# One fused kernel on one core: second block in halves, fewer float64 steps among the experts, expert 0's weights loaded later

## Chip, cores and metric

The kernel runs on one core of one Trainium2 chip. The metric is the device time of one launch in microseconds. Before the change the median of three runs is 641.63 us.

## What is computed

Three stages follow each other, on 2 x 768 tokens of 512 features.

```
x = attention(q, k, v)          # 2 batches, 8 heads, 768 positions, 64 features a head;
                                # a query sees the first n_global=8 keys and the last n_local=96
e = argmax(x @ w_gate); y = gate * relu(x @ w1[e]) @ w2[e]     # 8 experts, 512 -> 1024 -> 512
h = y @ w_in; g = max(h, 0) + log1p(exp(-|h|)); out = g @ w_out  # 512 -> 2048 -> 512, w_in, w_out float64
```

## The kernel before

**Attention.** The loop at L960 has one step `n` for each of 12 tiles x 8 heads (tile `i`, head `h`), plus eight steps to drain. A tile is 128 queries; tiles 0 and 6 are the first of a batch and see only their own keys, the others also the 96 keys before and the 8 global ones. In step `n` the scores of head `n` are multiplied (L720), the probabilities of head `n-4` transposed (L747), and in odd steps the heads `n-7` and `n-6` multiplied by v (L768). For the older keys L768 reads `vp`, which GpSimd fills in step 7 of the tile before (`prev_v`, L561 to L571; in a batch's second tile L570 also copies the global rows). q, k and v are loaded by SyncE (`load` at h = 1, `load_v` at h = 6). Each finished tile is routed (`route`, L792): x is transposed (L798, in step 8x+15), the expert chosen, and in step 8x+20 GpSimd scales the rows (L847) and scatters them to DRAM by an indirect DMA (L788, `scatter_x`). A scatter waits for the one before it. From tile 3 on there is a scatter in that step; step 7 of tiles 5, 6 and 7 issues one more, to catch up.

**Expert 0's parts.** L1011 calls `pump(-1, 0)` at step 4 of tiles 6 and 8; each call issues one half of expert 0's weights, two DMAs of 1 MB each (L405, L406, on SyncE's queue).

**Experts.** The loop at L1146 has 64 steps `s` (8 experts x 8 slices of the 1024 inner units) and two to drain: stage 1 of slice `s` (L1110), stage 2 of slice `s-2` (L1126). `pump` loads the weights of coming experts into five buffers. After four loads for the second block `load_x` (L1064) brings the last expert's rows, transposed at L1091.

**float64 weights.** `w_in` and `w_out` come as float64 words. `conv_step` (L487) turns one of 64 pieces (128 x 256) into float32: one store to DRAM (L492), one bit operation on VectorE (L80), one on ScalarE (L76) and two on VectorE (L77, L78), one load of a coming piece (L484). It runs twice a tile in attention from tile 5, once in each expert step from s = 6 (L1164), and twice in each step of the second block.

**Second block.** 1536 tokens in 3 chunks of 512, 2048 inner units in 8 blocks of 256, q0 to q7 (`Q2 = 8`). A step `x` of the plan (L1229) is one of 48 = 3 chunks x 16 slices: 12 matmuls of stage 1 (L1095 to L1097 through `three`, since each operand is split into a high and a low part), then 12 of stage 2 for step `x-2`. Chunk by chunk all 8 blocks are walked, forward, backward, forward. A block must be split into high and low before use: two raw loads (L462), four copies (L431 or L433) and four subtractions (L421). With five buffers, 14 blocks are loaded and split instead of 8. The output of a chunk stays in four PSUM banks through its 16 steps; `m_out` (L1215) then copies it (L1220 ScalarE, L1222 VectorE in turn) and scatters the rows to `out` (L1223). The last six steps run row block by row block (L1245).

What sets the order is the program: each engine takes its instructions in the order in which these loops issue them, and SyncE's and ScalarE's DMAs wait in those queues.

```
        if n in (6 * H + 4, 8 * H + 4):
            pump(-1, 0)
...
        if s >= 6:
            conv_step(1)
...
        return conv_done[0] >= 8 * (key[2] + 1)
```

Of the kernel before, what the change touches and what calls it, by code (L numbers as in the profile page):

```python
# [10 lines left out]
F32 = mybir.dt.float32  # L11
F32R = mybir.dt.float32r
# [4 lines left out]
ALU = mybir.AluOpType  # L17
# [5 lines left out]
P = 128  # L23
# [282 lines left out]
def fast_path(ctx, tc, q, k, v, n_global, n_local, w_gate, w1, w2, cap, w_in, w_out, out, const):  # L306
    nc = tc.nc
    B, H, S, D = q.shape
    T, DM = out.shape
    E, _, F = w1.shape  # L310
    F2 = w_in.shape[1]
# [3 lines left out]
    NTT = T // P  # L315
# [4 lines left out]
    Q2 = F2 // FQ  # L320
# [13 lines left out]
    rpool = ctx.enter_context(tc.tile_pool(name="rpool", bufs=3))  # L334
    cv = ctx.enter_context(tc.tile_pool(name="cv", bufs=2))

    xp = ctx.enter_context(tc.tile_pool(name="xp", bufs=1))
# [8 lines left out]
    uses = []  # L346
    for e in range(E):
        uses += [("e", e, i) for i in range(QE)]
    for c in range(T // 512):
        order = range(Q2) if c % 2 == 0 else range(Q2 - 1, -1, -1)  # L350
        uses += [("m", 0, i) for i in order]

    slot_of = {}
    use_buf = [None] * len(uses)
# [29 lines left out]
    NRAW = 4  # L384
# [95 lines left out]
    def conv_load():  # L480
        if conv:
            src, dst = conv.popleft()
            raw = cv.tile([P, FQ, 2], I32, name="cr", tag="cr", bufs=4)
            nc.scalar.dma_start(raw.rearrange("p n w -> p (n w)"), src)  # L484
            conv_raw.append((raw, dst))

    def conv_step(n):  # L487

        for _ in range(n):
            if conv_out:  # L490
                dst, t = conv_out.popleft()
                nc.scalar.dma_start(dst, f32(t))  # L492
                conv_done[0] += 1
            if conv_now:
                dst, t, u = conv_now
                words_to_f32(nc, t, u, None, None, 1)
                conv_out.append((dst, t))
                conv_now.clear()
            if conv_raw:
                raw, dst = conv_raw.popleft()  # L500
                t = cv.tile([P, FQ], I32, name="ct", tag="cq", bufs=5)
                u = cv.tile([P, FQ], F32, name="csq", tag="cu", bufs=2)
                words_to_f32(nc, t, u, raw[:, :, 1], raw[:, :, 0], 0)
                conv_now.extend([dst, t, u])
                conv_load()
# [454 lines left out]
    for n in range(NH + 8):  # L960
        i, h = divmod(n, H)
        if 0 <= n - 2 < NH:
            expo(n - 2)
        if 0 <= n - 1 < NH:
            if n <= H:
                make_bias0(n - 1)
            biased(n - 1)
            if n <= H:
                make_bias1(n - 1)
        if n < NH:  # L970
            scores(n)
        if 0 <= n - 4 < NH:
            transp(n - 4)
        if n % 2:
            for m in (n - 7, n - 6):
                if 0 <= m < NH:
                    pv(m)
        if n == H + 2:
            tri = strict_upper(nc, const, "tri", a2, ints, tag="here")
        if n < NH:  # L980
            if h == 1:
                load(i + 2)
            if h == (1 if i else 3):
                prep(i + 1, 0)
            if h % 2 and (i or h > 4) or i and h == 2:
                zero_fill(1)
            if h == (3 if i else 5):
                prep(i + 1, 1)
            if h == 6:
                load_v(i + 2)  # L990
                if i in (2, 3, 4):
                    conv_load()
            if h == 7:
                dup(i + 1)
                prev_v(i + 1)
                if i >= 5 and len(sc_q) > (i > 10):
                    scatter_x()
            if i >= 5 and h >= 6 and i < last:
                conv_step(1)
        for step, off in enumerate((15, 18, 20)):  # L1000
            x, r = divmod(n - off, H)
            if r == 0 and 0 <= x < last - 1:
                route(x, step)
        for step, at in enumerate((NH - 1, NH + 3, NH + 5)):
            if n == at:
                route(last - 1, step)
        if n == (last - 2) * H + 21:
            assert not sc_q
            moe_x["xr"] = ac.tile([P, 2, DM], F32, name="xr0")
            nc.sync.dma_start(moe_x["xr"], xs_d[0:FIRST, :].rearrange("(j p) d -> p j d", p=P))  # L1010
        if n in (6 * H + 4, 8 * H + 4):  # L1011
            pump(-1, 0)
    first_base(0)
    route(last, 0)
# [125 lines left out]
    LAG = 2  # L1140
# [5 lines left out]
    for s in range(len(steps) + LAG):  # L1146
        if s < len(steps):
            ui, f = steps[s]
            e_stage1(ui, f)
            if f in (3, 5, 6):  # L1150
                trans_x(ui + 1, (3, 5, 6).index(f))
            if f == 7 or s == 0:
                if s == 0:
                    load_order()
                load_x(ui + 1 + (f == 7))
        if s >= LAG:
            ui, f = steps[s - LAG]
            e_stage2(ui, f)
            if f % JE == JE - 1:
                done = ui * QE + f // JE  # L1160
        pump(done, 2 if s > 2 else 0, s % 2 == 0)
        if 1 <= s <= 4:
            next(routed, None)
        if s >= 6:  # L1164
            conv_step(1)


    NCH = T // 512
    plan = []
    for c in range(NCH):  # L1170
        for s in range(Q2):
            u = UM + c * Q2 + s
            for j in range(2):
                plan.append((c, u, 2 * s + j, j))
    NF2 = F2 // P
    gs_, os_ = {}, {}

    def m_stage1(x):
        c, u, f, j = plan[x]
        w = w_of(u)[0]  # L1180
        ps = bank("A", "ps_m")
        sl = slice(c * 512, (c + 1) * 512)
        for d in range(NC):
            three(ps, w[:, 0, d, j * P:(j + 1) * P], w[:, 1, d, j * P:(j + 1) * P], zh[:, d, sl], zl[:, d, sl],
                  d == 0, d == NC - 1)
        a = cv.tile([P, 512], F32, name="sa", tag="sa", bufs=2)
        nc.scalar.activation(a, ps, AF.Abs)  # L1187
        nc.scalar.activation(a, a, AF.Exp, scale=-1.0)
        nc.scalar.activation(a, a, AF.Ln, bias=1.0)  # L1189
        nc.vector.scalar_tensor_tensor(a, in0=ps, scalar=0.0, in1=a, op0=ALU.max, op1=ALU.add)  # L1190
        y = x - (len(plan) - TAIL)
        if 0 <= y < 4:
            if y % 2 == 0:
                gs_["two"] = (mo if y // 2 else xp).tile([P, 4, 512], F32R, name="g2", tag=f"x{y // 2}", bufs=1)
            gh, gl_ = gs_["two"][:, y % 2, :], gs_["two"][:, 2 + y % 2, :]
        else:
            g = mo.tile([P, 2, 512], F32R, name="g", tag="h", bufs=3)
            gh, gl_ = g[:, 0, :], g[:, 1, :]
        nc.vector.tensor_copy(gh, a)  # L1199
        nc.vector.tensor_tensor(gl_, a, f32(gh), op=ALU.subtract)  # L1200
        gs_[x] = (gh, gl_)

    def m_stage2(x, ts_=range(4)):
        c, u, f, j = plan[x]
        w = w_of(u)[1]
        if f == 0:
            os_[c] = [bank("BBCC"[t], "ps_o") for t in range(4)]
        gh, gl_ = gs_[x]
        for t in ts_:
            three(os_[c][t], gh[:, t * P:(t + 1) * P], gl_[:, t * P:(t + 1) * P], w[:, 0, j, :], w[:, 1, j, :],  # L1210
                  f == 0, f == NF2 - 1)
            if f == NF2 - 1:
                m_out(c, t)

    def m_out(c, t):  # L1215
        if t % 2 == 0:
            os_[c, "o"] = mo.tile([P, 2, 512], F32, name="o", tag="m4", bufs=2)
        o = os_[c, "o"][:, t % 2, :]
        if t % 2:
            nc.scalar.copy(o, os_[c][t])  # L1220
        else:
            nc.vector.tensor_copy(o, os_[c][t])  # L1222
        nc.gpsimd.indirect_dma_start(  # L1223
            out=out, out_offset=bass.IndirectOffsetOnAxis(ap=ids_sb[:, 4 * c + t:4 * c + t + 1], axis=0), in_=o,
            in_offset=None, bounds_check=T - 1, oob_is_err=False)
# [2 lines left out]
    slow = None  # L1228
    for x in range(len(plan)):  # L1229
        m_stage1(x)  # L1230
        conv_step(1)
        if LAG <= x < len(plan) - TAIL + LAG:
            m_stage2(x - LAG)
            if (x - LAG) % 2 == 1:
                done = plan[x - LAG][1]
        conv_step(1)
        pump(done, 2)
        if x < NTT:
            scatter_ids(x)
        if x == NTT:  # L1240
            nc.sync.dma_start(ids_sb, ids_d.rearrange("(j p) o -> p (j o)", p=P))
        if x == 2 * NF2:
            slow = nc.values_load(slow_i[0:1, 0:1], min_val=0, max_val=1,
                                  skip_runtime_bounds_check_because="one minus a minimum of comparisons")
    for t in range(4):  # L1245
# [46 lines left out]
```

## Time and profile before

| | us |
|---|---|
| median of 3 runs | 641.63 |
| lowest, highest run | 638.79, 643.66 |
| the profiled execution, its own time | 643.61 |
| its span | 641.7 |
| TensorE matmul busy in the span | 622.5 |
| VectorE, ScalarE, GpSimd busy | 308.1, 266.9, 122.6 |

The span is what the profile shows; 1.9 us of the execution's time lie around it. Attention fills about the first 150 us of the span, the experts reach to about 367, the second block to the end.

### The profile page before, as it was taken

The numbers are of one execution on the slowest core, as the hardware profiler recorded it, in microseconds if no ns is written. First come the engines' busy times: TensorE is split into PE (matmuls) and PEld (weight loads), VectorE is DVE, ScalarE is ACT, GpSimd is POOL, SyncE is SP. The second block draws the span as 40 slices with busy tenths as digits, with TensorE's granted clock in tenths as the row PEclk, the third lists the DMA queues.
The fourth block names the chain that finished last, engine by engine and source line by source line (L and its number), as shares of the span: only waits on it lengthen the run. The fifth ranks groups of instructions, "written<-read, shape, count | busy, mean of one in ns | idle before, by whom it ended". The sixth has DMA issues, their size and how long they took to land. (4 is left out here: it accounts for less than half of the span.)

```text
span 641.7 us, 9519 instructions
## 1 busy us (share of the span) xinstructions
PE 622.5 (97%) x3257; PEld 535.9 (84%) x3257; DVE 308.1 (48%) x939; ACT 266.9 (42%) x570; POOL 122.6 (19%) x152
## 2 busy tenths in 40 slices
PE   6999979999999999999999999999999999999996
PEld 4899979998876788999989978888888888888874
DVE  7766868955031233343466354533345433455340
ACT  4565746742222223333344354433445333344340
POOL 3231443311000000000022432531042100142001
PEclk9999979989999999999999999999999999999999
DMA  8758898413995677899996432540023200011001
GB/s 170 209 173 228 228 271 268 148 51 112 386 387 193 190 254 277 288 316 316 309 345 200 148 48 34 105 71 12 1 95 93 76 0 1 33 66 34 1 1 69
DMA packets 94666, 99.61 MB, mean 155 GB/s; under 512 B 44790, under 2 KB 60162, under 8 KB 94610
## 3 DMA queue, kind: packets, MB, share of 16 engines
q1 hardware_dynamic: 73874, 67.45, 36.7%
q10 hardware_dynamic: 18432, 25.17, 11.6%
q0 software_dynamic: 2304, 6.30, 2.6%
q8 instruction: 28, 0.46, 0.3%
q14 instruction: 28, 0.23, 0.1%
HBM read 78.44 MB, written 20.46 MB: 154 GB/s over the span
## 5 line engine op out<-in xcount | busy, mean ns | idle before, releaser
L1126 PE MATMUL ps_y<-h,w 128*128 128x256 f32 (+7 forms) x512 | 115.0, 368 | 0.0
L1110 PE MATMUL ps_h<-xT,w 128*128 128x256 f32 (+7 forms) x512 | 114.7, 368 | 0.0
L1110 PEld LDWEIGHTS ps_h<-xT,w 128*128 128x128 f32 x512 | 93.3, 190 | 12.1 <-ACT xT L1080 0.2
L1126 PEld LDWEIGHTS ps_y<-h,w 128*128 128x128 f32 x512 | 92.0, 190 | 10.7
L1190 DVE SCALAR_TENSOR_TENSOR sa<-ps_m,sa 128x512 f32<-128x512 f32 x48 | 33.2, 692 | 132.7 <-ACT sa L1189 132.7
L1187 ACT ACTIVATE sa<-ps_m 128x512 f32<-128x512 f32 x48 | 28.8, 600 | 137.3 <-PE ps_m L1097 136.2
L1112 ACT ACTIVATE h<-ps_h 128x256 f32<-128x256 f32 (+7 forms) x64 | 23.8, 373 | 139.7 <-PE ps_h L1110 120.1
L1095 PE MATMUL ps_m<-zh,w1s 128*128 128x512 f32 x192 | 75.9, 395 | 0.0
L1097 PE MATMUL ps_o<-w2s,g 128*128 128x512 f32 x192 | 75.7, 394 | 0.0
L1096 PE MATMUL ps_m<-zl,w1s 128*128 128x512 f32 x192 | 75.7, 394 | 0.0
L1096 PE MATMUL ps_o<-w2s,g 128*128 128x512 f32 x192 | 75.5, 393 | 0.0
L1097 PE MATMUL ps_m<-zh,w1s 128*128 128x512 f32 x192 | 75.3, 392 | 0.0
L1095 PE MATMUL ps_o<-w2s,g 128*128 128x512 f32 x192 | 74.8, 389 | 0.0
L80 DVE SCALAR_TENSOR_TENSOR ct<-csq,ct 128x256 int32<-128x256 int32 x64 | 29.2, 457 | 78.0 <-ACT csq L76 76.7
L421 POOL TENSOR_TENSOR w1s<-raw,w1s 128x512 fp32r<-128x512 f32 x19 | 24.9, 1321 | 212.6 <-ACT w1s L433 212.5
L736 ACT ACTIVATE s_sb<-s_sb,negm 128x232 f32<-128x232 f32 (+1 forms) x96 | 44.7, 473 | 36.7 <-DVE negm L729 36.1
L720 PE MATMUL ps_s<-kwin,qpad 128*128 128x232 f32 (+1 forms) x192 | 56.4, 381 | 2.1 <-DVE negm L729 2.0
L1095 PEld LDWEIGHTS ps_m<-zh,w1s 128*128 128x128 f32 x192 | 36.0, 188 | 9.3 <-DVE sa L1190 1.0
L1096 PEld LDWEIGHTS ps_o<-w2s,g 128*128 128x128 f32 x192 | 36.0, 188 | 8.7
L1095 PEld LDWEIGHTS ps_o<-w2s,g 128*128 128x128 f32 x192 | 36.1, 188 | 8.4 <-DVE g L1199 0.3
L1097 PEld LDWEIGHTS ps_m<-zh,w1s 128*128 128x128 f32 x192 | 36.0, 188 | 8.4
L1097 PEld LDWEIGHTS ps_o<-w2s,g 128*128 128x128 f32 x192 | 36.0, 188 | 8.1 <-DVE g L1200 0.4
(185 smaller groups left out, 919.3 us busy)
## 6 DMA issues: line engine op xcount, KB each, us to landing
w<-in_moe_w_dram SPq DMA_DIRECT2D x32, 1024.0 KB
cr<-in_moe_w_in_dram ACTq DMA_DIRECT2D x32, 256.0 KB
cr<-in_moe_w_out_dram ACTq DMA_DIRECT2D x32, 256.0 KB
raw<-wi_d SPq DMA_DIRECT2D x14, 512.0 KB
raw<-wo_d SPq DMA_DIRECT2D x14, 512.0 KB
xs_d<-early SPq DMA_DIRECT2D x22, 256.0 KB
wi_d<-ct ACTq DMA_DIRECT2D x32, 128.0 KB
wo_d<-ct ACTq DMA_DIRECT2D x32, 128.0 KB
```

Of the source, the lines that this page charges most:

```text
L80: nc.vector.scalar_tensor_tensor(t, in0=u.bitcast(I32), scalar=3, in1=t, op0=ALU.logical_shift_left, op1=ALU.bitwise_or)
L421: eng.tensor_tensor(lo, raw, f32(hi), op=ALU.subtract)
L720: nc.tensor.matmul(ps[:, :w], tr[i][h % 2][:, h // 2, :], kwin[t % 2][:, h // 2, c0:], start=True, stop=True)
L736: nc.scalar.activation(pt_[n][:, :w], pt_[n][:, :w], AF.Exp, bias=negm[:, n:n + 1], scale=-1.0)
L1095: nc.tensor.matmul(ps, hi_l, hi_r, start=first, stop=False)
L1096: nc.tensor.matmul(ps, hi_l, lo_r, start=False, stop=False)
L1097: nc.tensor.matmul(ps, lo_l, hi_r, start=False, stop=last)
L1110: nc.tensor.matmul(ps, w[:, c, j * P:(j + 1) * P], xt_[ui][:, c, :], start=c == 0, stop=c == NC - 1)
L1112: nc.scalar.activation(h[:, :n], ps, AF.Relu)
L1126: nc.tensor.matmul(ys[ui, d], w[:, j, d * P:(d + 1) * P], h, start=f == 0, stop=f == NFE - 1)
L1187: nc.scalar.activation(a, ps, AF.Abs)
L1190: nc.vector.scalar_tensor_tensor(a, in0=ps, scalar=0.0, in1=a, op0=ALU.max, op1=ALU.add)
```

## The change

- The second block is walked in halves of the inner units. `segs` lists six segments of 8 steps: chunks 0, 1, 2 with blocks q0 to q3, then chunks 2, 1, 0 with q4 to q7. In this order each block is loaded and split once (8 instead of 14).
- Chunk 2 keeps its PSUM banks through both halves. Chunks 0 and 1 are copied to SBUF after their first half (`m_keep`, ScalarE and VectorE in turn), and `m_out` adds that copy on VectorE at the end of their second half.
- Among the experts `conv_step` runs in even steps only, in the second block once a step.
- `load_v` is called at h = 5 instead of 6 (the `conv_load` of tiles 2 to 4 stays at h = 6).
- Expert 0's two parts are pumped at step 4 of tiles 9 and 10 instead of 6 and 8.
- The four `g` tiles of the tail use the buffers of the raw loads.

```diff
+    segs = []
+    for half in range(2):
+        for c in range(NCH) if half == 0 else range(NCH - 1, -1, -1):
+            qs = range(half * Q2 // 2, (half + 1) * Q2 // 2)
+            segs.append((c, half, qs if (len(segs) + half * NCH) % 2 == 0 else qs[::-1]))
+    for _, _, qs in segs:
+        uses += [("m", 0, i) for i in qs]
...
-            if h == 6:
+            if h == 5:
                 load_v(i + 2)
-                if i in (2, 3, 4):
-                    conv_load()
+            if h == 6 and i in (2, 3, 4):
+                conv_load()
...
-        if n in (6 * H + 4, 8 * H + 4):
+        if n in (9 * H + 4, 10 * H + 4):
             pump(-1, 0)
...
-        if s >= 6:
+        if s >= 6 and s % 2 == 0:
             conv_step(1)
...
         if 0 <= y < 4:
+            g = rpool.tile([P, 2, 512], F32R, name="g2", tag="raw", bufs=NRAW)
...
+        on = c == NCH - 1
+        if first and not (on and half):
             os_[c] = [bank("BBCC"[t], "ps_o") for t in range(4)]
...
             three(os_[c][t], gh[:, t * P:(t + 1) * P], gl_[:, t * P:(t + 1) * P], w[:, 0, j, :], w[:, 1, j, :],
+                  first and not (on and half), end and not (on and not half))
+            if end and half:
                 m_out(c, t)
+            elif end and not on:
+                m_keep(c, t)
...
+        if t == 0:
+            kept[c] = (mo if c else xp).tile([P, 4, 512], F32, name="kept", tag=f"x{c}", bufs=1)
+        if t % 2:
+            nc.scalar.copy(kept[c][:, t, :], os_[c][t])
+        else:
+            nc.vector.tensor_copy(kept[c][:, t, :], os_[c][t])
...
+        if c in kept:
+            nc.vector.tensor_tensor(o, os_[c][t], kept[c][:, t, :], op=ALU.add)
+        elif t % 2:
...
         m_stage1(x)
-        conv_step(1)
         if LAG <= x < len(plan) - TAIL + LAG:
```

## Rows read from the trace of the kernel before

**Rows 1.** The page's first part: busy time, share, instructions of each engine.

```profile
PE 622.5 (97%) x3257; PEld 535.9 (84%) x3257; DVE 308.1 (48%) x939; ACT 266.9 (42%) x570; POOL 122.6 (19%) x152
```

**Rows 2.** Waits of TensorE in the span: total us, times, longest.

```profile
PE ps_pv L768 <- POOL vp L571: 3.1, 1, 3.1
...
PE ps_xt L1091 <- DMA xr<-xs_d: 1.6, 1, 1.6
```

**Rows 3.** Stretches of 4 us; columns as in the first line.

```profile
core 0: us, PE busy (x) PEld busy (x) DVE busy (x) ACT busy (x) POOL busy (x), PEclk, DMA share, GB/s
...
84.00:88.00 4.00, 1.63 (x12) 1.27 (x10) 3.86 (x18) 2.81 (x7) 1.40 (x2) 0.95 1.23 266
88.00:92.00 4.00, 3.30 (x14) 3.18 (x15) 1.21 (x4) 0.44 (x1) 3.18 (x3) 0.50 0.75 246
...
112.00:116.00 4.00, 4.00 (x34) 3.76 (x33) 3.88 (x12) 2.91 (x7) 3.26 (x4) 1.00 0.54 154
...
140.00:144.00 4.00, 4.00 (x22) 4.00 (x22) 3.10 (x24) 1.11 (x3) 0.00 (x0) 0.50 0.01 2
```

**Rows 4.** A stretch of 40 us of the second block, same columns.

```profile
380.00:420.00 40.00, 40.00 (x175) 32.54 (x174) 20.20 (x31) 17.68 (x30) 14.21 (x12) 1.00 0.47 82
```

**Rows 5.** Timeline of TensorE: the transposes of L798, one set a tile.

```profile
67.61 0.61 PE L798 MATMUL ps_xT<-ident,x 128*128 128x128 f32 x4
...
76.88 0.61 PE L798 MATMUL ps_xT<-ident,x 128*128 128x128 f32 x4
...
90.47 1.06 PE L798 MATMUL ps_xT<-ident,x 128*128 128x128 f32 x4
...
103.07 0.61 PE L798 MATMUL ps_xT<-ident,x 128*128 128x128 f32 x4
...
113.74 0.60 PE L798 MATMUL ps_xT<-ident,x 128*128 128x128 f32 x4
```

**Rows 6.** Timeline of GpSimd: start, us; in brackets the idle time before.

```profile
72.25 0.98 POOL L788 DMA_INDIRECT xs_d<-xg,sl  x1 [3.00 <-DMA xs_d<-xg,sl]
...
79.19 1.02 POOL L788 DMA_INDIRECT xs_d<-xg,sl  x1 [2.49 <-DMA xs_d<-xg,sl]
...
86.58 1.40 POOL L570 COPY vp<-vt 8x520 f32<-8x520 f32 x2 [5.84 <-issue]
88.03 0.61 POOL L571 COPY vp<-vt 96x520 f32<-96x520 f32 x1
```

**Rows 7.** Scatters of L788, issue to landing: all twelve, the one at 72.3, the one at 79.2.

```profile
DMA to landing us min/median/max: 2.7/4.9/7.3
...
DMA to landing us min/median/max: 6.2/6.2/6.2
...
DMA to landing us min/median/max: 7.3/7.3/7.3
```

**Rows 8.** Timeline of SyncE's queue in attention.

```profile
72.77 0.39 SPq L405 DMA_DIRECT2D w<-in_moe_w_dram  x1
...
96.42 0.39 SPq L406 DMA_DIRECT2D w<-in_moe_w_dram  x1
...
113.62 0.31 SPq L540 DMA_DIRECT2D vt<-in_v_dram  x1
...
136.20 0.39 SPq L1010 DMA_DIRECT2D xr<-xs_d  x1
```

**Rows 9.** SyncE's waits from 300 to 420 us, and its timeline there.

```profile
SPq L462 <- DMA wi_d<-ct: 6.4, 1, 6.4
...
326.44 1.09 SPq L1072 DMA_DIRECT2D xr<-xs_d  x2
```

**Rows 10.** Groups of instructions in the second block: busy us, mean ns.

```profile
L1190 DVE SCALAR_TENSOR_TENSOR sa<-ps_m,sa 128x512 f32<-128x512 f32 x48 | 33.2, 692 | 132.7 <-ACT sa L1189 132.7
...
L421 POOL TENSOR_TENSOR w2s<-raw,w2s 128x512 fp32r<-128x512 f32 x15 | 19.4, 1296 | 31.0 <-ACT w2s L433 14.3 <-issue 6.4 <-SPq L1258 5.3
...
L1220 ACT COPY o<-ps_o 128x512 f32<-128x512 f32 x6 | 3.5, 582 | 15.0 <-PE ps_o L1097 15.0
```

More of the change, by code (lines that the diff above doesn't have):

```diff
@@ L348, in fast_path @@
         uses += [("e", e, i) for i in range(QE)]
-    for c in range(T // 512):
-        order = range(Q2) if c % 2 == 0 else range(Q2 - 1, -1, -1)
-        uses += [("m", 0, i) for i in order]
+    NCH = T // 512
+    segs = []
[5 more added lines that the diff above has]
+        uses += [("m", 0, i) for i in qs]
     slot_of = {}
@@ L1163, in fast_path @@
             next(routed, None)
-        if s >= 6:
+        if s >= 6 and s % 2 == 0:
             conv_step(1)
-    NCH = T // 512
     plan = []
-    for c in range(NCH):
-        for s in range(Q2):
-            u = UM + c * Q2 + s
+    for k, (c, half, qs) in enumerate(segs):
+        for i in range(len(qs)):
             for j in range(2):
-                plan.append((c, u, 2 * s + j, j))
-    NF2 = F2 // P
+                e = 2 * i + j
+                plan.append((c, half, UM + k * len(qs) + i, j, e == 0, e == 2 * len(qs) - 1))
     gs_, os_ = {}, {}
     def m_stage1(x):
-        c, u, f, j = plan[x]
+        c, _, u, j = plan[x][:4]
         w = w_of(u)[0]
@@ L1192, in m_stage1 @@
         if 0 <= y < 4:
-            if y % 2 == 0:
-                gs_["two"] = (mo if y // 2 else xp).tile([P, 4, 512], F32R, name="g2", tag=f"x{y // 2}", bufs=1)
-            gh, gl_ = gs_["two"][:, y % 2, :], gs_["two"][:, 2 + y % 2, :]
+            g = rpool.tile([P, 2, 512], F32R, name="g2", tag="raw", bufs=NRAW)
         else:
             g = mo.tile([P, 2, 512], F32R, name="g", tag="h", bufs=3)
-            gh, gl_ = g[:, 0, :], g[:, 1, :]
+        gh, gl_ = g[:, 0, :], g[:, 1, :]
         nc.vector.tensor_copy(gh, a)
@@ L1203, in m_stage2 @@
     def m_stage2(x, ts_=range(4)):
-        c, u, f, j = plan[x]
+        c, half, u, j, first, end = plan[x]
         w = w_of(u)[1]
-        if f == 0:
+        on = c == NCH - 1
+        if first and not (on and half):
             os_[c] = [bank("BBCC"[t], "ps_o") for t in range(4)]
@@ L1210, in m_stage2, with m_keep @@
             three(os_[c][t], gh[:, t * P:(t + 1) * P], gl_[:, t * P:(t + 1) * P], w[:, 0, j, :], w[:, 1, j, :],
-                  f == 0, f == NF2 - 1)
-            if f == NF2 - 1:
+                  first and not (on and half), end and not (on and not half))
+            if end and half:
                 m_out(c, t)
+            elif end and not on:
+                m_keep(c, t)
+    kept = {}
+    def m_keep(c, t):
+        if t == 0:
[4 more added lines that the diff above has]
+            nc.vector.tensor_copy(kept[c][:, t, :], os_[c][t])
     def m_out(c, t):
@@ L1218, in m_out @@
         o = os_[c, "o"][:, t % 2, :]
-        if t % 2:
+        if c in kept:
+            nc.vector.tensor_tensor(o, os_[c][t], kept[c][:, t, :], op=ALU.add)
+        elif t % 2:
             nc.scalar.copy(o, os_[c][t])
@@ L1234, in fast_path @@
             if (x - LAG) % 2 == 1:
-                done = plan[x - LAG][1]
+                done = plan[x - LAG][2]
         conv_step(1)
@@ L1241, in fast_path @@
             nc.sync.dma_start(ids_sb, ids_d.rearrange("(j p) o -> p (j o)", p=P))
-        if x == 2 * NF2:
+        if x == 2 * NTT:
             slow = nc.values_load(slow_i[0:1, 0:1], min_val=0, max_val=1,
```

## Prediction, made before the result was known

> **What bounds the kernel now.** I read the page's first part, then stretches, then TensorE's waits, then the timelines around the longest wait. TensorE is busy for 622.5 of 641.7 us [rows 1], so an edit that only unloads VectorE, ScalarE, GpSimd or the DMAs saves nothing by itself: only idle TensorE time, and time at the lower clock, can be had. In the second block there is none. Five stretches of 40 us from 380 to 580 each show 40.00 busy with 175 matmuls, two chunk ends among them [rows 4]. A step of 24 matmuls takes 24 x 40/175 = 5.49 us, and the change keeps all 48 steps. The two waits of TensorE that the change can reach are 3.1 us in attention, for `vp`, and 1.6 us among the experts, for rows from DRAM [rows 2].
>
> The first is dearer than it looks. In 84 to 88 us TensorE is busy for 1.63 of 4 us, and in the next 4 us its granted clock is 0.50, the lower level, 1.2 GHz [rows 3]. The transposes of L798 come once a tile and measure it: a full tile takes 113.74 - 103.07 = 10.67 us, the light one at the change of batch 76.88 - 67.61 = 9.27, but the two around the wait 13.59 and 12.60 [rows 5]. The first of these is partly light too, so I hold it against 9.27: 4.32 + 1.93 = 6.25 us lost; against 10.67 for both it would be 4.85.
>
> **Expert 0's parts moved.** Why was `vp` late? L571 ended at 88.64; TensorE had wanted it from 88.7 - 3.1 = 85.6. L571 stands behind L570 on GpSimd, which began at 86.58 after 5.84 us for which the profile names no releaser [rows 6]. The scatter issued at 79.19 took 7.3 us to land [rows 7], so it landed at 86.5, 0.1 us earlier. I take that as the releaser: the next scatter must wait for it, and the wait seems to have been placed ahead of the copies. That scatter had itself waited for the one of 72.25, which took 6.2 us [rows 6, 7]. Right there, at 72.77, SyncE issued the first 2 MB of expert 0 [rows 8]; in 84 to 88 the DMA share is 1.23 [rows 3].
>
> Without those 2 MB, with a landing time L for both scatters: the second is issued at 72.25 + L + 0.74 (79.19 less 78.45), lands L later, and the copies are done 0.1 + 2.06 us after that: 75.15 + 2L. TensorE waits only if this passes 85.6, so if L is over 5.2. The median of the twelve is 4.9, from 2.7 to 7.3 [rows 7], and the slow end lies beside this load. I take L = 4.9, no wait, and with no wait no lower clock there: -6.25 us. Bounds: 0 (L near 7) and -6.25.
>
> What do the parts cost at tiles 9 and 10? On SyncE's queue the first now comes behind tile 11's q and k and just ahead of its v load, which is issued at 113.62 before the change [rows 8]; the second follows at once, because SyncE runs ahead and nothing of tile 10 is left to load. Ahead of the next user of that queue, the load at 136.20 [rows 8], lie over 20 us; 4.2 MB at the 266 GB/s of a crowded stretch need 16, and in 112 to 116 only 154 GB/s are moved [rows 3]. v of tile 11 is read 18 steps, or 24 us (10.67/8 a step), after its issue. The scatters there come a tile (10.67 us) apart, without a second one on their heels, so one of 7.3 us still lands before the next. The nearest evidence is the old second part, its last DMA issued at 96.42 [rows 8]: the tile after it took its 10.67 us [rows 5]. So 0, with 0 and 6.25 per tile (what the old first part cost) as ends; nothing could be gained there, as TensorE doesn't idle in it.
>
> One rule of the Trainium skill speaks against this edit. The page "DMA: Bandwidth & Descriptors", section "Issuing engines are not separate DMA queues", says that DMAs started by SyncE, ScalarE or GpSimd end up on the same 16 engines and interleave. The slow scatter beside SyncE's load agrees (7.3 against 2.7 us). By the rule alone the delay only moves, to the scatters of tiles 9 and 10, and the sum below would lack its first term.
>
> **v loads one step earlier.** The order of SyncE's DMAs is the same (a zero-fill of step 5 before, one of step 7 behind), and the load waits for the same products with v, of step 5. 0, within 0.3 either way, a tenth of the one wait for `vp`.
>
> **float64 steps thinned among the experts.** Of TensorE's idle time there only the 1.6 us count [rows 2]; freed VectorE and ScalarE time saves nothing. The late rows are loaded at 326.44, behind a raw load before which SyncE stood 6.4 us for a float64 store [rows 9]. With a store every second step that store lies further back and the DMAs are emptier; a load a few us earlier removes the wait. I take -1.6, between 0 and -1.6.
>
> The price is lateness. Attention converts 12 pieces and the experts 30 more instead of all 52. A block needs 8 pieces more than the one before it, and a piece is stored two calls after its first. q0 to q3 are stored by s = 48 and q4 by s = 64, before use; q7 by x = 23, is split at x = 24 and 25 and used from x = 30: 5 x 5.49 = 27 us to spare. q5 and q6 are stored before their buffers come free, and have about as much. ScalarE may stand at a copy whose raw load has just been issued, which costs nothing as it works some 16 of 40 us [rows 4]. 0; each step of lateness past x = 30 would cost 5.5.
>
> **Halves; each block split once.** Six blocks less are 24 copies and 24 subtractions less, of up to 1.296 us on GpSimd [rows 10]. They lie beside TensorE's unbroken work [rows 4]: 0. New are eight copies (`m_keep`) and eight additions. Chunk ends at which banks are reused go from two to four. Between a chunk's last matmul and the first that needs its third bank lie 12 + 6 matmuls, 4.1 us; four additions in a row on VectorE at 0.692 (nearest: L1190, which also reads PSUM and SBUF [rows 10]) are 2.8 us, most of it while the banks are still being filled. 0; without that cover one addition at each of four ends, 2.8. On the path to the end stands only the last one: 0.692 in place of ScalarE's 0.582 [rows 10], +0.1.
>
> **Sum.** From the profiled execution's own 643.61 us (span 641.7 and 1.9 around it): -6.25 - 1.6 + 0.1 gives 635.9. That execution lies 2.0 above the median, 641.63, near the top of runs from 638.79 to 643.66. A second stretch at the lower clock, 140 to 144 [rows 3], isn't touched; it costs about 3 us (half of some 6) where it occurs, and could make part of that spread. I can't tell how much of the 2.0 the changed kernel keeps, and take 0.5 off: 635.4 us.
>
> **Rivals.**
> - *The wait shrinks only.* With L = 6.2, as at 72.25, the copies end at 87.55 and TensorE waits 2.0 instead of 3.1 us; in proportion 4.0 of the 6.25 stay: 639.4. For it: L must stay under 5.2 and its median is 4.9, twice in a row. Against: 6.2 was reached with the load in flight. 0.18.
> - *The loads hurt at the new place.* If `vp` or v of tiles 10 and 11 comes late at both as it did at tile 7, 12.5 us come on top: 647.9, slower than before. It decides where a scatter holds the copies past TensorE's need; with one scatter a tile instead of two back to back, one landing of some 6 us less stands in the way. 0.05. The section of the Trainium skill named above leads here.
> - *The late rows stay late*, because SyncE is held by something else: 637.0. 0.10.
> - *The second stretch at the lower clock goes too*, since the tail of attention falls 6 us earlier: 632.4. The profile can't tell. 0.12.
> - *The halves and the single split do what they say and move no time*: part of the forecast. That they cost, by 2.8 us at the chunk ends, would give 638.2, and lies within the range.
>
> **How the numbers follow.** The forecast has 0.55, its own range 633.5 to 637. A measurement of this kernel tells about 1% from no change, that is 6.4 us: 635.2 and 648.0. Faster by over 1%: somewhat under half of the forecast and its bounds to the low side (0.28) and the rival at 632.4 (0.12), 0.40. Slower by over 1%: the upper half of the second rival and what I have not thought of, 0.04. The rest, 0.56, is within 1%. The range 631 to 641 takes in all but the rival at 647.9 and the outer ends.
>
> **What would show it.** Right: no idle TensorE between 75 and 95 us with a clock of 1.00, L798's intervals 9.3 and about 10.7 in place of 13.59 and 12.60; no wait at L1091; 175 matmuls in every 40 us of the second block; L421 32 times instead of 56. Wrong: a wait for `vp` or ps_pv after 100 us; TensorE idle at a chunk end or at L1095 for a split; the lower clock at a new place.

## Result, and the profile after

The changed kernel is slower, by half a per cent: median 645.01 us of 22 runs against 641.50 of 22 of the kernel before, ratio 1.0051, 95% interval [1.0028, 1.0074]. Forecast was 635.4, from 631 to 641. The profiled execution of the changed kernel took 644.8 us (span 642.9) against 643.61 (641.7). Function for function the new line numbers are 4 to 18 higher: L804 is the old L798, L577 the old L571, L1101 to L1103 the three matmuls, L1191 to L1194 the old L1187 to L1190, L1258 the load of `ids_sb`.

I cut both traces at the first matmul of the experts, at the first of the second block and at the last of all. Attention got shorter by 5.0 us (it ends at 146.27 instead of 151.28), the experts by 1.3 (216.32 instead of 217.64), and the second block longer by 7.4 (273.85 instead of 266.45). The second stretch at the lower clock, at the end of attention, lasted 6.8 us in both. So the gain came, and something unforeseen took more back. The page's first part answers [rows 1]: as much TensorE work, less on the other engines.

```profile
PE 622.3 (97%) x3257; PEld 535.6 (83%) x3257; DVE 300.0 (47%) x933; ACT 256.7 (40%) x552; POOL 102.0 (16%) x136
```

TensorE's waits over the whole span answer [rows 2]:

```profile
PE ps_m L1101 <- DVE sa L1194: 5.4, 1, 5.4
PE ps_prep L698 <- POOL vp L610: 4.1, 1, 4.1
...
PE ps_xt L1097 <- DMA xr<-xs_d: 0.3, 1, 0.3
```

The 3.1 us for `vp` at the old L768 are gone, the 1.6 us for the late rows have become 0.3, and there is a new wait of 5.4 us at the first matmul of a step of the second block, for VectorE. (The 4.1 us of the second line lie at the start of the kernel and are there before the change too.) Around tile 7, to be read against [rows 3, 5], with the same columns:

```profile
80.00:84.00 4.00, 3.45 (x28) 3.03 (x26) 3.71 (x16) 1.79 (x6) 1.07 (x2) 1.00 0.93 242
84.00:88.00 4.00, 4.00 (x29) 3.68 (x30) 3.43 (x21) 3.10 (x9) 3.38 (x4) 1.00 0.40 114
88.00:92.00 4.00, 4.00 (x33) 3.82 (x33) 3.31 (x12) 2.77 (x7) 2.09 (x3) 1.00 0.90 257
```

```profile
77.26 0.61 PE L804 MATMUL ps_xT<-ident,x 128*128 128x128 f32 x4
...
87.38 0.60 PE L804 MATMUL ps_xT<-ident,x 128*128 128x128 f32 x4
...
98.06 0.60 PE L804 MATMUL ps_xT<-ident,x 128*128 128x128 f32 x4
```

The clock stays at 1.00, and the two intervals are 10.12 and 10.68 us instead of 13.59 and 12.60. Stretches of the second block, to be read against [rows 4]:

```profile
core 0: us, PE busy (x) PEld busy (x) DVE busy (x) ACT busy (x) POOL busy (x), PEclk, DMA share, GB/s
380.00:420.00 40.00, 40.00 (x175) 32.49 (x174) 23.47 (x51) 16.81 (x31) 7.21 (x7) 1.00 0.61 102
...
424.00:428.00 4.00, 4.00 (x19) 3.26 (x18) 2.08 (x5) 0.00 (x0) 0.97 (x1) 1.00 0.05 2
428.00:432.00 4.00, 4.00 (x19) 3.23 (x19) 0.00 (x0) 0.00 (x0) 0.97 (x1) 1.00 0.01 0
432.00:436.00 4.00, 3.12 (x14) 2.22 (x12) 0.00 (x0) 0.00 (x0) 0.00 (x0) 1.00 0.14 1
436.00:440.00 4.00, 0.00 (x0) 0.00 (x0) 0.22 (x1) 2.11 (x5) 0.00 (x0) 0.70 0.69 199
440.00:444.00 4.00, 3.47 (x8) 2.80 (x9) 3.69 (x9) 2.30 (x5) 0.00 (x0) 0.50 0.47 135
444.00:448.00 4.00, 4.00 (x18) 3.24 (x18) 2.19 (x5) 2.18 (x4) 0.00 (x0) 0.94 0.28 94
448.00:488.00 40.00, 40.00 (x175) 32.52 (x174) 24.76 (x49) 18.95 (x35) 4.16 (x3) 1.00 0.27 83
```

Read it down the columns of zeros: ScalarE does nothing from 424 to 436, VectorE nothing from 428 to 436, TensorE nothing from 436 to 440, and then TensorE runs at the lower level, 1.2 GHz. On both sides of the hole stand the 175 matmuls of before. ScalarE stood for 14.3 us, 11 more than the up to 3.3 that it idles in a step; matmuls whose operands were ready hid some 5.6 of them. The price is the rest, 5.4 us, and nine matmuls at the lower clock (3.97 us from the first to the tenth instead of 2.08, so 1.9), together 7.3 of the 7.4 us by which the block is longer.

Who stood first? The timeline of ScalarE (ACTq is its DMA queue):

```profile
422.61 0.63 ACT L1193 ACTIVATE sa<-sa 128x512 f32<-128x512 f32 x1
422.67 0.33 ACTq L498 DMA_DIRECT2D wi_d<-ct  x1
423.15 0.41 ACT L76 ACTIVATE csq<-cr 128x256 f32<-128x256 f32 x1
437.45 0.34 ACTq L490 DMA_DIRECT2D cr<-in_moe_w_in_dram  x1
437.83 0.60 ACT L1191 ACTIVATE sa<-ps_m 128x512 f32<-128x512 f32 x1 [14.26 <-DMA ids_sb<-ids_d]
```

The activation at 437.83 is named as the waiting instruction, but ahead of it in the same queue stands the load of the next float64 piece (L490), which `conv_step` issues. In the steps around it such a load goes out within 0.7 us of the store (L498); here 14.8 us behind it. The profile names as releaser (what ended the wait) a DMA with which this load has no data in common: the load of the token numbers, `ids_sb`, which SyncE issues. SyncE's queue shows when:

```profile
402.30 0.36 SPq L468 DMA_DIRECT2D raw<-wo_d  x1
433.21 0.36 SPq L1258 DMA_DIRECT2D ids_sb<-ids_d  x1
```

and its waits from 360 to 460 us why:

```profile
SPq L1258 <- DMA ids_d<-tokid,pos_i: 30.5, 1, 30.5
```

`ids_sb` must wait for the twelve scatters of `scatter_ids`, one after the other on GpSimd. First and last of them:

```profile
370.18 1.26 POOL L927 DMA_INDIRECT ids_d<-tokid,pos_i  x1 [0.16 <-issue]
...
430.15 0.97 POOL L927 DMA_INDIRECT ids_d<-tokid,pos_i  x1 [2.28 <-DMA ids_d<-tokid,pos_i]
```

In the records of the two DMAs the link can be read. Each DMA signals a completion semaphore, a counter that tells when its data has landed. Both DMAs signal the same one, number 105, and ahead of the ScalarE load at 437.45 stands a wait for it. The last signal of the `ids_sb` load comes at 437.37, and the wait ends within 0.05 us of that. In this program semaphores 101 to 108 are given to the DMAs of SyncE and of ScalarE together, and a DMA that gets a number waits until its last holder has landed, whichever engine issued that; the DMAs of GpSimd signal 111 to 118. The kernel before has the same load and a wait of SyncE for the same scatters:

```profile
SPq L1241 <- DMA ids_d<-tokid,pos_i: 15.6, 1, 15.6
```

But there ScalarE issues no DMA in the second block, since all 64 pieces were converted before it.

Theory A: this coupling is the whole loss, and a gain of the forecast's size lies behind it. Against it stood that the halves, the thinned conversion or the moved loads cost time in themselves. Theory D concerns the other side: that the wait for `vp` was worth less than I had put it at, because it is not in every execution of the kernel before.

### The profile page after: what moved, and what is told of

It reads as the page before. It is cut to its first block, busy times and chain, and to the rows that moved or that the text cites. A ratio compares the mean times of both kernels' runs of the same rounds, so it can differ in the third digit from the quotient of the medians.

```text
span 642.9 us, 9399 instructions
## 1 busy us (share of the span) xinstructions
PE 622.3 (97%) x3257; PEld 535.6 (83%) x3257; DVE 300.0 (47%) x933; ACT 256.7 (40%) x552; POOL 102.0 (16%) x136
## 5 line engine op out<-in xcount | busy, mean ns | idle before, releaser
L1194 DVE SCALAR_TENSOR_TENSOR sa<-ps_m,sa 128x512 f32<-128x512 f32 x48 | 33.2, 691 | 124.8 <-ACT sa L1193 124.8
L1191 ACT ACTIVATE sa<-ps_m 128x512 f32<-128x512 f32 x48 | 28.8, 600 | 144.8 <-PE ps_m L1103 130.6
L1101 PE MATMUL ps_m<-zh,w1s 128*128 128x512 f32 x192 | 76.8, 400 | 5.4 <-DVE sa L1194 5.4
L1103 PE MATMUL ps_m<-zh,w1s 128*128 128x512 f32 x192 | 76.0, 396 | 0.0
L1103 PE MATMUL ps_o<-w2s,g 128*128 128x512 f32 x192 | 75.7, 394 | 0.0
L1101 PE MATMUL ps_o<-w2s,g 128*128 128x512 f32 x192 | 74.7, 389 | 0.0
L80 DVE SCALAR_TENSOR_TENSOR ct<-csq,ct 128x256 int32<-128x256 int32 x64 | 31.2, 488 | 80.4 <-ACT csq L76 80.1
L427 POOL TENSOR_TENSOR w1s<-raw,w1s 128x512 fp32r<-128x512 f32 x11 | 15.2, 1391 | 260.6 <-ACT w1s L439 260.6
L1101 PEld LDWEIGHTS ps_m<-zh,w1s 128*128 128x128 f32 x192 | 36.6, 190 | 15.2 <-DVE sa L1194 6.8
L1103 PEld LDWEIGHTS ps_m<-zh,w1s 128*128 128x128 f32 x192 | 36.4, 190 | 8.6
L1102 PEld LDWEIGHTS ps_o<-w2s,g 128*128 128x128 f32 x192 | 36.0, 188 | 8.7
L1101 PEld LDWEIGHTS ps_o<-w2s,g 128*128 128x128 f32 x192 | 36.1, 188 | 8.4 <-DVE g L1201 0.3
L1102 PEld LDWEIGHTS ps_m<-zl,w1s 128*128 128x128 f32 x192 | 36.4, 190 | 7.9
```

Source lines behind the costliest of these rows:

```text
L80: nc.vector.scalar_tensor_tensor(t, in0=u.bitcast(I32), scalar=3, in1=t, op0=ALU.logical_shift_left, op1=ALU.bitwise_or)
L427: eng.tensor_tensor(lo, raw, f32(hi), op=ALU.subtract)
L1101: nc.tensor.matmul(ps, hi_l, hi_r, start=first, stop=False)
L1102: nc.tensor.matmul(ps, hi_l, lo_r, start=False, stop=False)
L1103: nc.tensor.matmul(ps, lo_l, hi_r, start=False, stop=last)
```

## Experiments on the loss

**1. Conversion in each expert step again**, so that ScalarE has no load left in the second block:

```diff
-        if s >= 6 and s % 2 == 0:
+        if s >= 6:
             conv_step(1)
```

> The changed kernel with the float64 step back in every step among the experts (the rest of the change stays). Theory A: in the changed kernel ScalarE stands 14.3 us in the second block because its load of a float64 piece has to wait for the load of the row numbers (ids_sb), which itself waits for twelve scatters; TensorE loses 7.4 us by it (second block 273.9 us against 266.5 before). With all pieces converted before the second block ScalarE issues no DMA there: no wait at the softplus, second block 266.5, about 645.0 - 7.4 = 637.6 us. Rival B: the halves and the copies of partial sums cost the 7.4 us: the wait stays and the time is about 645.

637.57 us, ratio to the kernel before 0.9947 [0.9918, 0.9976]. The second block takes 266.46 us, ScalarE's waits hold no DMA, and SyncE's waits from 360 to 460 us are:

```profile
SPq L468 <- DVE w1s L427: 60.0, 2, 49.3
SPq L1258 <- DMA ids_d<-tokid,pos_i: 48.2, 1, 48.2
```

SyncE stands at `ids_sb` even longer, 48.2 us instead of 30.5, and the second block is as short as before the change. So it isn't SyncE's wait that costs, but what hangs on its end. The wait for late rows is 1.9 us here.

**2. The load of `ids_sb` later**, when ScalarE's last load has long gone out (458.62):

```diff
-        if x == NTT:
+        if x == 26:
             nc.sync.dma_start(ids_sb, ids_d.rearrange("(j p) o -> p (j o)", p=P))
```

> The changed kernel with the load of the row numbers issued at x = 26 instead of 12, after the last float64 piece (x = 23) and before its first use (x = 33); the thinned float64 steps stay. Theory A: the wait is gone although the pieces are still converted in the second block: second block 266.5, about 637.6 us. Rival C: it is the float64 work itself in the second block (ScalarE, VectorE and DMA time between the softplus) that costs: the time stays near 645 here, while the kernel with the steps back among the experts is faster.

635.39 us (634.03 to 638.21), 0.9913 [0.9882, 0.9944]: one number in one line takes 9.6 us off the changed kernel by the medians, and 8.9 by the two ratios (the kernel before has a median of 641.50 beside the result and of 640.24 here). The load is issued at 488.69, where the scatters are long done, and the second block takes 266.44 us. TensorE has no listed wait left in it. ScalarE's waits from 360 to 460 us:

```profile
ACT sa L1191 <- PE ps_m L1103: 47.0, 16, 3.3
ACT csq L76 <- DVE ct L77: 2.5, 3, 1.2
ACT sa L1191 <- DVE ct L80: 2.0, 1, 2.0
```

ScalarE now waits for TensorE, as it should.

**3. The same load at the same place, issued by GpSimd.** If it is the load itself or its time that hurts, this changes nothing; if it is the semaphores that SyncE and ScalarE share, it removes the stall.

```diff
-            nc.sync.dma_start(ids_sb, ids_d.rearrange("(j p) o -> p (j o)", p=P))
+            nc.gpsimd.dma_start(ids_sb, ids_d.rearrange("(j p) o -> p (j o)", p=P))
```

> The changed kernel with the load of the row numbers still at x = 12 but issued from GpSimd's queue instead of SyncE's. Theory A, sharper: ScalarE's and SyncE's DMAs take turns on the same few completion semaphores, and a DMA isn't issued before the last one of its turn has landed; a load on GpSimd's queue has a semaphore of another set, so ScalarE doesn't stand: second block 266.5, about 635.5 us as with the late load. Rival E: it is the load's own slowness (four bytes a row) or its place in time that blocks the other DMAs: ScalarE stands 14 us as before, 643 to 645.

635.54 us, 0.9919 [0.9893, 0.9945]; second block 266.44. GpSimd issues it at 435.93, 2.7 us later than SyncE did in the changed kernel, and ScalarE's queue goes on beside it:

```profile
435.93 1.08 POOL L1258 DMA_DIRECT2D ids_sb<-ids_d  x1 [4.79 <-DMA ids_d<-tokid,pos_i]
```

```profile
435.75 0.60 ACT L1191 ACTIVATE sa<-ps_m 128x512 f32<-128x512 f32 x1 [3.29 <-PE ps_m L1103]
...
437.06 0.33 ACTq L498 DMA_DIRECT2D wo_d<-ct  x1
437.52 1.43 ACTq L490 DMA_DIRECT2D cr<-in_moe_w_in_dram  x1
```

With conversion and load both where they were, only the issuing engine changed, and the stall is gone. SyncE's later loads go out earlier too, as nothing holds that queue at `ids_sb`; but in experiment 1 it stands there for 48.2 us, and the second block is as short. Theory A is shown by three ways round it.

The page "DMA: Bandwidth & Descriptors" of the Trainium skill (section "Issuing engines are not separate DMA queues") says that DMAs of several engines run on the same 16 engines, and that starting them from several engines saves only sequencer time. For the transfers nothing here speaks against it. Here the choice of the issuing engine was worth more: it decided whose landing a queue waits for, 14.3 us of ScalarE's time.

**4. Halves and single split alone**: the changed kernel with the other three edits taken back.

```diff
-            if h == 5:
+            if h == 6:
                 load_v(i + 2)
...
-        if n in (9 * H + 4, 10 * H + 4):
+        if n in (6 * H + 4, 8 * H + 4):
...
-        if s >= 6 and s % 2 == 0:
+        if s >= 6:
```

> The kernel before with the halves alone (each block split once, copies of partial sums, additions at the end, g tiles of the tail in the raw buffers, one float64 call a step in the second block, where nothing is left to convert); expert 0's parts, the float64 steps among the experts and the v load as before. Theory A: TensorE's second block stays 266.5 us, since the dropped splits and the new copies all lie beside it: 640.2 to 641.5 us, no change. Rival B: the four chunk ends cost up to 0.7 us each: second block 269, 643 to 644.

640.32 us, 1.0001 [0.9967, 1.0035]; second block 266.42 us, and

```profile
380.00:420.00 40.00, 40.00 (x175) 32.54 (x174) 14.70 (x25) 14.38 (x24) 9.10 (x9) 1.00 0.02 4
```

for it and the next four stretches of 40 us alike 175 matmuls. The new order costs nothing and brings nothing. This run also holds the one edit that the list of the change leaves out, the read of `slow` at step 24 instead of 32 (`2 * NTT` in place of `2 * NF2`).

## Experiments on the gain

**5. The move of expert 0's parts alone**, in the kernel before:

```diff
-        if n in (6 * H + 4, 8 * H + 4):
+        if n in (9 * H + 4, 10 * H + 4):
```

> The kernel before with one edit: expert 0's parts at tiles 9 and 10. Theory A: the wait of TensorE for vp goes and the lower clock after it; the profiled executions differ by 5.0 us there (first expert matmul 151.3 before, 146.3 after), so 641.5 - 5.0 = 636.5 us. Rival D: the profiled execution of before was 2.1 us slower than the median because its wait was longer than usual, and a usual run gains less: 638.5 to 640. No change at all (641.5) would say that the gain in the profile was chance.

638.15 us, 0.9963 [0.9935, 0.9992]: 2.4 us, not 6.25. Its profiled execution (643.61) lies at the top of its runs and shows that a clock loss elsewhere can hide the gain. Stretches of it at the end of attention:

```profile
core 0: us, PE busy (x) PEld busy (x) DVE busy (x) ACT busy (x) POOL busy (x), PEclk, DMA share, GB/s
130.00:134.00 4.00, 3.51 (x32) 3.13 (x30) 0.76 (x3) 2.36 (x5) 0.00 (x0) 1.00 0.51 177
134.00:138.00 4.00, 4.00 (x23) 4.00 (x23) 3.08 (x23) 1.11 (x3) 0.00 (x0) 0.54 0.03 9
138.00:142.00 4.00, 4.00 (x20) 4.00 (x19) 0.72 (x7) 0.58 (x1) 0.97 (x1) 0.50 0.17 66
142.00:146.00 4.00, 4.00 (x12) 2.88 (x12) 2.12 (x16) 1.12 (x3) 0.47 (x1) 0.50 0.00 0
146.00:150.00 4.00, 4.00 (x15) 3.19 (x14) 3.19 (x18) 1.17 (x2) 0.50 (x1) 0.75 0.17 66
```

and the same stretches of experiment 2, which had its lowest run profiled:

```profile
130.00:134.00 4.00, 3.52 (x32) 3.13 (x30) 0.85 (x4) 2.03 (x5) 0.00 (x0) 1.00 0.42 153
134.00:138.00 4.00, 3.75 (x35) 3.59 (x35) 3.44 (x27) 1.59 (x4) 0.51 (x1) 1.00 0.01 2
138.00:142.00 4.00, 3.37 (x19) 2.50 (x19) 2.52 (x19) 1.12 (x3) 0.55 (x2) 1.00 0.17 66
```

The work up to 134 us is alike (3.51 and 3.52 us busy); then the granted clock falls to 1.2 GHz for 13.7 us in one and not at all in the other. This is the second low stretch of [rows 3]. Over all twelve profiles it lasted 0 us (once), 3.4 (six times), 6.8 (four times) and 13.7 (once), with no edit that goes with it: twice the kernel before was profiled, and it had 6.8 and 3.4.

**6. The changed kernel with the parts at their old place**, the stall left in:

```diff
-        if n in (9 * H + 4, 10 * H + 4):
+        if n in (6 * H + 4, 8 * H + 4):
```

> The changed kernel with expert 0's parts back at tiles 6 and 8. Theory A: the wait for vp at tile 7 is back beside the wait in the second block: 645.0 + 5.0 = 650 us (by rival D 647 to 648.5). If the earlier load of v has a part in the attention's gain, the wait for vp is smaller than the 3.1 us of before and the time nearer 645.

650.90 us, 1.0126 [1.0068, 1.0184]: 5.9 us more than the changed kernel by the medians, 4.8 by the ratios. Its profile has the wait for `vp` (2.3 us), and the stall.

**7. The same edit without the stall.**

```diff
-        if n in (9 * H + 4, 10 * H + 4):
+        if n in (6 * H + 4, 8 * H + 4):
...
-        if x == NTT:
+        if x == 26:
```

> The changed kernel with the load of ids_sb at x = 26 instead of 12 (as in e2_ids_late) and with expert 0's parts back at step 4 of tiles 6 and 8. It prices the move beside everything else of the change. If the move is worth what the prediction said (6.25 us), this takes 635.4 + 6.3 = 641.7; if it is worth the 2.4 us of e3_move_only, 637.8; if it is worth the 5.9 us by which the kernel after and e5 differ, 641.3. The profile should show 266.4 us for the second block and no wait of ScalarE for ids_sb in every case, and the wait for vp either at 2 to 3 us or not at all, with the transposes of L798 at tile 7 some 12 to 13 us apart with it and 10 to 11 without.

640.37 us, 0.9996 [0.9967, 1.0025]: 5.0 us more than experiment 2 by the medians, 5.3 by the ratios, and no better than the kernel before. In the profiled execution, the fastest of its twelve, there is no wait for `vp`. So without the move no gain is left that the interval can tell. Alone the move measured 2.4 us, beside the others some 5. Why it is worth less alone stays open; the intervals are about 2 us either way (nearly 4 in experiment 6), and that of experiment 5 reaches to 0.9935, 4.2 us.

**8. The kernel before, profiled again.**

> The kernel before, unchanged, looked at once more. Theory: the wait for vp at tile 7 is there in some executions only. The first profile had it at 3.1 us, with intervals of 13.59 and 12.60 us of L798; two variants with the same order of work in attention had none. If it is in every execution, this profile has a wait of 2 to 4 us and an execution near 643; if only in some, it may have none, with intervals near 10.9 and 10.7 and an execution near 637 to 639.

638.24 us, and TensorE's waits from 75 to 95 us are

```profile
PE ps_pv L768 <- POOL vp L571: 0.5, 1, 0.5
PE ps_pv L768 <- DVE negm L729: 0.4, 1, 0.4
```

half a microsecond instead of 3.1, with no lower clock behind it. L798's intervals at tiles 6 and 7 are 10.48 and 10.67 instead of 13.59 and 12.60. Theory D holds: the wait on which my largest term rests is in some executions only. The table sets it beside the two scatters ahead of the copies:

| | parts at | first scatter lands after | second issued | lands after | L570 begins | `vp` done | wait | interval |
|---|---|---|---|---|---|---|---|---|
| before, first profile | 6, 8 | 6.2 | 79.19 | 7.3 | 86.58 | 88.64 | 3.1 | 13.59 |
| experiment 6 | 6, 8 | 5.9 | 78.69 | 6.8 | 85.60 | 87.59 | 2.3 | 12.85 |
| before, again | 6, 8 | 3.8 | 76.64 | 7.5 | 84.25 | 86.12 | 0.5 | 10.48 |
| experiment 7 | 6, 8 | 3.7 | 77.19 | 7.4 | 84.68 | 86.56 | none | 10.37 |
| experiment 9 | 6, 8 | 3.7 | 76.63 | 7.3 | 84.08 | 85.94 | none | 10.31 |
| experiment 5 | 9, 10 | 3.5 | 76.90 | 6.0 | 83.00 | 84.85 | none | 10.16 |
| after | 9, 10 | 3.2 | 77.27 | 5.6 | 82.93 | 84.79 | none | 10.12 |

With the parts at tile 6 the first scatter lands after 6 us or after 3.8, and the waits of 2 to 3 us stand only with the former. The second scatter takes 6.8 to 7.5 us with the parts there and 5.6 to 6.0 without. Over all twelve profiles, the six with the parts at tile 6 have waits for `vp` of 3.1, 2.3, 1.0 (experiment 4, where the profile names a load, but `vp` is done at 86.56 and the matmul begins at 86.61), 0.5 and twice none, and the six with the parts at tiles 9 and 10 none. In all seven rows L570 begins 0.1 us after the second scatter's landing. Two rows of GpSimd, from the second profile of the kernel before:

```profile
76.64 1.02 POOL L788 DMA_INDIRECT xs_d<-xg,sl  x1 [0.17 <-POOL xg L847]
...
84.25 1.20 POOL L570 COPY vp<-vt 8x520 f32<-8x520 f32 x2 [5.92 <-issue]
```

**9. No catch-up scatter in tile 6**, in the kernel before: if L570 stands because the wait of the scatter issued after the copies is placed ahead of them, this frees it.

```diff
-                if i >= 5 and len(sc_q) > (i > 10):
+                if i >= 5 and i != 6 and len(sc_q) > (i > 10):
                     scatter_x()
```

> The kernel before, expert 0's parts at tiles 6 and 8, but without the catch-up scatter in step 7 of tile 6 (a later one takes its rows). Theory A: the copies for vp (L570, L571) stood behind the wait of that scatter for the scatter before it, which the load made slow; without it the copies run early, TensorE doesn't wait for vp, the L798 intervals are 10.1 and 10.7 instead of 13.6 and 12.6: about 638.2 us, like the moved load alone. Rival G: the load delays vp in another way (v or the scores late): the intervals stay near 13 and the time at 640 to 641.5.

641.26 us, 0.9992 [0.9960, 1.0025]: no gain. And the reason fell: the scatter behind the copies is gone, and L570 still begins only when the one before has landed:

```profile
76.63 1.02 POOL L788 DMA_INDIRECT xs_d<-xg,sl  x1 [0.17 <-POOL xg L847]
...
84.08 1.19 POOL L570 COPY vp<-vt 8x520 f32<-8x520 f32 x2 [5.90 <-issue]
85.33 0.61 POOL L571 COPY vp<-vt 96x520 f32<-96x520 f32 x1
85.93 1.63 POOL L847 TENSOR_SCALAR xg<-x,ga 128x512 f32<-128x512 f32 x1
87.73 1.05 POOL L788 DMA_INDIRECT xs_d<-xg,sl  x1 [0.17 <-issue]
```

The records show what holds the copies until that landing: a wait instruction of L570's own. In the first profile of the kernel before it is the longer of two (shortest, median and longest in ns, then first and last start):

```profile
L570 POOLq EVENT_SEMAPHORE  x2: 17/3748/7479, 15.4 to 79.0; - x2
```

It lasts from 79.02 to 86.50 and waits for semaphore 113, which the scatter issued at 79.19 signals for the last time at 86.47 (the other semaphore it names, of a v load, had its signals by 70). In all twelve profiles this wait ends 0.02 to 0.03 us after the scatter's last signal. So the copies wait for the scatter ahead of them, whichever scatter follows. Why the program places that wait there, though copies and scatter share no data, isn't shown.

**10. `load_v` back at h = 6**, on top of experiment 2:

```diff
-            if h == 5:
+            if h == 6:
                 load_v(i + 2)
```

> The changed kernel with the row numbers loaded at x = 26, and the v load back at h = 6. Theory: the order of the DMAs is the same, so nothing changes: 635.4 us, L798 intervals 10.0 and 10.7. Rival F: the earlier v load shares in the attention's gain (with expert 0's parts at the old place TensorE waited 2.3 instead of 3.1 us): a wait for vp is back in part and the time is 1 us or more above.

636.97 us, 0.9918 [0.9889, 0.9946], against 0.9913 of experiment 2. SyncE's DMAs stand in the same order in both traces, and in neither does TensorE wait for `vp` at tile 7. 0 within the intervals, as forecast.

## Why the prediction was wrong

- *Expert 0's parts moved* (-6.25). The mechanism is right: `vp` waits for the second scatter's landing, and without the parts there is no wait and no lower clock at tile 7 [rows 3, 5]. Only the reason for it, the next scatter's wait, was wrong (experiment 9). L was 3.2 and 5.6 instead of 4.9 twice, a sum 1.0 smaller. Nothing hurt at tiles 9 and 10, as the second rival had it. The delay did move there, though: the longest landing of the twelve, 7.4 us, is now that of the scatter issued at 108.24, beside the second part (109.25), but TensorE waits for nothing there. The size was wrong in two ways. I held the first interval against 9.27, and without the wait it is 10.12: TensorE is busy for 3.45 of 4 us from 80 to 84 even so. The two intervals thus gave 3.47 + 1.92 = 5.4, all of attention 5.0. And it was the size of one execution. I had seen that it lay 2.0 us above the median and took off 0.5; over many executions the term is 2.4 (alone) to some 5.
- *v loads one step earlier* (0), *halves; each block split once* (0): right. The subtractions of L427 are 32, and the `kept` copies and additions lie beside TensorE's work. The 0.1 of the last addition came: 6.1 instead of 6.0 us from the last matmul to the end of the span.
- *float64 steps thinned*, the gain (-1.6): right in kind, 1.6 became 0.3 in the changed kernel; experiments 1 and 2 differ by 2.2 us in their medians, with overlapping intervals, and have 1.9 against 0.2 us of this wait.
- *float64 steps thinned*, the price: this is the step that failed. "ScalarE may stand at a copy whose raw load has just been issued, which costs nothing as it works some 16 of 40 us", and "0; each step of lateness past x = 30 would cost 5.5": I reckoned when each piece is ready and found no piece late, which is true. I didn't count the instructions that the moved steps issue. Each `conv_step` also puts a store and a load on ScalarE's queue; moved into the second block they come to stand beside SyncE's load of `ids_sb`, with which they share completion semaphores, and that load hangs on twelve scatters. Measured: 14.3 us of ScalarE, 5.4 of TensorE, 7.4 us in the length of the block. By the medians the stall is worth 9.6 us (645.01 - 635.39), by the ratios 8.9; with intervals of about 2 us this doesn't tell whether it costs more than the 7.4 of the traces.
- *Late rows stay late*, *the loads hurt at the new place*, *the wait shrinks only*: none came. *The second low stretch goes too*: it comes and goes by itself, so it was not the change's to move.

Without the stall the sum was right: 635.4 forecast, 635.39 and 635.54 measured in experiments 2 and 3, though partly by luck: the sum started at 643.1, 1.6 above the median of 641.50, and the move is worth less than 6.25. The trace of before held the warning: SyncE waits there for the same scatters at `ids_sb`, 15.6 us, harmlessly. I had read TensorE's waits in the second block, found none, and stopped. Of the signs that were to show the forecast wrong, the last one came: the lower clock at a new place.

The fastest versions are those of experiments 2 and 3 (0.9913 and 0.9919 of the kernel before), and 10, which differs from 2 in the v load alone.

## What to carry to other kernels

When a step is moved past another engine's DMA, list its DMA issues too and ask which landings each must wait for: a queue can stand for a DMA that shares no data with it, and the profile shows it as a releaser that has no business there. A DMA that hangs on a long chain is best issued after its chain has ended, or from a queue on which nothing urgent shares its completion semaphores. A wait read from a single execution is one draw: take a second profile before pricing it, above all where that execution lies off the median.

## What was not expected of the hardware

- The lower clock at the end of attention comes for 0, 3.4, 6.8 or 13.7 us from profile to profile, 6.8 and 3.4 in two of the same kernel; in the two set side by side above, TensorE was as busy just ahead of it (3.51 and 3.52 us of 4). The last interval of L804 is 7.11 us without it (experiment 2) and 8.8 with 6.8 us of it (the changed kernel). The spread of the runs goes with the granted clock: of 24 runs of the kernel before, taken beside experiment 9, the fastest (636.70) has a mean of 0.999 and the slowest (646.07) of 0.984.
- The same 256 KB scatter beside the same loads landed after 6.2 us in one execution of the kernel before and after 3.8 in another.
